# A new hand-written order of all steps in a fused sliding-window attention and expert kernel

## The chip, the cores and the metric

The kernel runs on one core of one Trainium2 chip. The metric is device time in microseconds (us). Before the change it was 203.53 us, the median of three runs (203.12 to 203.67).

## What is computed

Eight batches of eight heads go through causal attention with a window of 64 positions (576 positions, head dimension 64). The result, laid out as 576 rows of 512 per batch, goes through one of eight experts. The expert is chosen per batch from the mean of the batch's own attention output, so its weights cannot be fetched before that batch's attention is done.

```python
scores = scale * np.matmul(q, k.transpose(0, 1, 3, 2))
mask = (rel >= 0) & (rel < window)
scores = np.where(mask, scores, -1000000000.0)
...
x = np.ascontiguousarray(attn_out.transpose(0, 2, 1, 3)).reshape(B, S, H * D)
...
pooled = x.mean(axis=1)
logits = pooled @ w_gate
e_idx = np.argmax(logits, axis=1)
...
    h = np.maximum(x[mask] @ w1[e], 0.0)
    out[mask] = gate_w[mask, None, None] * (h @ w2[e])
```

## The kernel before

**Units.** Attention is cut into 40 units, five per batch: unit 5b+i with i below 4 is two heads by the first 512 positions of batch b, and unit 5b+4 is the last 64 positions of all eight heads (the tail). A unit goes through these steps, each one letter of the order, with the unit's number behind it:

- T (L214): 16 transposes on PE (8 for a tail) of q and then k, loaded as bf16, into one PSUM tile `tp`. A small m puts the tile into the pool `ps_m`, else it is in `ps_t`, which has one buffer.
- U and k (L238, L249): copies of the q half and of the k half out of PSUM into `qt` and `kT`. A small a puts the copy on ACT, a small d on DVE.
- S (L257): 16 small matmuls that give the scores. With m they go into two tiles of `ps_m`, else into the one tile of `ps_s`. With b, two mask matmuls (L269) come first and put -30000 outside the window, so that no mask is needed afterwards.
- E (L279): the exponential on ACT. It is one instruction for `ps_s` (L288) and two for `ps_m` (L291).
- K (L295): the mask as a multiplication on DVE, for units without b.
- l, n, R (L303, L347, L354): row sums on PE into the one buffer `lb`, then logarithm and exponential on ACT, which give the reciprocal.
- A and X (L318, L360): the product with v on PE, and the scaling on DVE into `xm`, which also sums for the gate.

**Batches.** Q (L104) loads q (even number) or k (odd number) of a batch; L (L137) loads one of five parts of v, t (L130) the tails of q and k, V (L148) copies v into a shifted form on DVE. g, j, G, H, I (L378 to L439) compute the gate; P (L411) reads the chosen expert's number into a register of POOL, and W (L416) loads one of four pieces of that expert's weights: 4b and 4b+1 are the halves of w1, 4b+2 and 4b+3 those of w2.

**Expert.** Each c takes the next of 18 chunks per batch: eight chunks of w1 (L461, 8 matmuls each), one for the tail rows (L470), eight half chunks of w2 (L503, 8 matmuls each) and one for the tail (L512). Chunk tiles share the three buffers of `ps_m` with the m variants above. ra and rd empty the next finished chunk on ACT or on DVE; O stores a finished output tile from POOL's queue, o from SP's (for a tail, half from SP's and half from ACT's, L492).

**What sets the order.** Nothing is scheduled automatically: the tuple OPS is a list of some 890 such letters, and each letter issues its instructions at that place on every engine that it touches. Each engine works through its own part strictly in that order. All loads and nearly all stores go through POOL's one queue, whose transfers land in the order of their issue. `ld` has three buffers for q and for k, `vw` three for v, and `w1b` and `w2b` three each (`WSLOT`, L98).

**The start.** Half of the heads of q and k of batch 0 come from POOL (heads 4 to 7 as "48", heads 0 and 1 as "02"), while heads 2 and 3 ("24") are loaded as float32 by SP (Y, L116) and cast on chip (C, L123).

```python
    with tc.manual_schedule():
        for op in OPS:
            c, x = op[0], op[1:].lstrip("abdm")
            e = op[1:len(op) - len(x)]
            if c == "c":
                todo.pop(0)()
            elif c in "oO":
                store(nc.sync if c == "o" else nc.gpsimd)
            elif c == "r":
                evac.pop(0)(e)
```

## Time and profile before

| | |
|---|---|
| time, median of three | 203.53 us |
| span of the profiled execution | 201.92 us |
| so around the span | 1.61 us |
| first transpose on PE | 6.88 us |
| first matmul of an expert (L461) | 40.84 us |
| last matmul issued (L512) | 196.54 us, a group of 16 |

The profiled execution is one run, and its own time outside the profiler is not told: its span and the 1.61 us that separate it from the median stand for it. All times below are counted from the span's start. A row of the timeline begins with start and duration; a row of the list of windows gives busy time per engine in that stretch; a row of the list of DMAs gives size and the time from issue to landing.

### The profile page before, as it was taken

How to read it: one execution, taken by the hardware profiler on the slowest of the kernel's cores; microseconds unless marked ns; L12 is line 12 of the kernel's file. 1: busy time of each engine (PE TensorE's matmuls, PEld its weight loads, DVE VectorE, ACT ScalarE, POOL GpSimd, SP SyncE). 2: the span in 40 equal slices, each digit the busy share in tenths (PEclk: the TensorE clock that was granted, in tenths of full speed). 3: DMA queues.
4: the chain of work that ended last, by engine and by line, in shares of the span. 5: the costliest groups of instructions: out<-in, count | busy, mean ns of one | idle time of the engine just before them, and what ended most of it. 6: DMA issues, size and time to landing. Idle time of an engine off the chain costs nothing.

```text
span 201.9 us, 8105 instructions
## 1 busy us (share of the span) xinstructions
PE 183.5 (91%) x3518; PEld 124.2 (62%) x3522; DVE 119.9 (59%) x347; ACT 131.8 (65%) x247; POOL 111.0 (55%) x158
## 2 busy tenths in 40 slices
PE   0487886899999999999999999999999999999991
PEld 0455564656677756577667666676656666776760
DVE  3527989595477546895877457966494651216410
ACT  2179998876599578977779975757787436321121
POOL 7985939235931593478633552439452716553561
PEclk9999999999999999999999999999999999999998
DMA  6999999999999999999999999999999999999693
GB/s 135 175 188 159 194 162 198 199 198 174 196 201 197 170 198 193 174 201 167 200 206 200 169 195 223 259 208 137 183 237 243 266 254 212 274 212 301 235 325 134
DMA packets 83346, 41.16 MB, mean 204 GB/s; under 512 B 48080, under 2 KB 80976, under 8 KB 83312
## 3 DMA queue, kind: packets, MB, share of 16 engines
q0 software_dynamic: 81936, 39.72, 138.5%
q1 hardware_dynamic: 768, 0.85, 1.3%
q8 instruction: 27, 0.44, 0.8%
q10 hardware_dynamic: 608, 0.08, 0.2%
q14 instruction: 7, 0.06, 0.1%
HBM read 61.88 MB, written 9.44 MB: 353 GB/s over the span
## 4 chain that ended last, share of the span: by engine, by line
PE 77%; DMA 9%; POOL 7%; issue 3%; DVE 2%; ACT 1%; POOLq 0%; DVEq 0%; ACTq 0%
PE ph L461 28%; PE po L503 25%; DMA vw<-in_v_dram 9%; PE tp L225 5%; PE ph L470 4%; PE s L275 4%; PE av L331 3%; PE po L512 3%; PE lb L309 3%; POOL vw L141 2%; POOL km L110 2%; POOL qm L110 1%; POOL out_dram L492 1%; PE gps L392 1%; POOL qkt L133 1%
## 5 line engine op out<-in xcount | busy, mean ns | idle before, releaser
L503 PE MATMUL po<-w2b,hm 128*64 128x512 f16 x512 | 60.1, 379 | 0.0
L461 PE MATMUL ph<-xm,w1b 128*64 128x512 f16 x512 | 60.0, 379 | 0.0
L461 PEld LDWEIGHTS <-w1b 128*64 128x64 f16 x512 | 31.7, 110 | 18.7 <-issue 0.4
L503 PEld LDWEIGHTS <-hm 128*64 128x64 f16 x512 | 30.1, 110 | 19.3
L141 POOL DMA_DIRECT2D vw<-in_v_dram x32 | 28.9, 910 | 13.3 <-DMA w1b<-in_moe_w_dram 4.3
L446 ACT ACTIVATE hm<-ph,gw 128x512 f16<-128x512 f32 x39 | 26.6, 693 | 13.4 <-PE ph L461 13.3
L492 POOL DMA_DIRECT2D out_dram<-ob x31 | 17.2, 557 | 25.0 <-DMA w1b<-in_moe_w_dram 7.0
L351 ACT ACTIVATE ln<-lb 128x512 f32<-128x512 f32 (+1 forms) x40 | 22.5, 563 | 11.8 <-PE lb L309 8.6
L364 DVE CUSTOM_DVE_ANT_0 xm<-av,rl 128x512 f16<-128x512 f32 x32 | 21.6, 686 | 10.4 <-PE av L331 9.5
L482 ACT COPY ob<-po 128x512 f32<-128x512 f32 x18 | 10.6, 586 | 23.6 <-PE po L503 23.6
L448 DVE TENSOR_SCALAR hm<-ph,gw 128x512 f16<-128x512 f32 x25 | 18.7, 748 | 12.1 <-PE ph L461 11.6
L357 ACT ACTIVATE rl<-ln 128x512 f32<-128x512 f32 (+1 forms) x40 | 23.3, 594 | 1.5 <-DVE pool L364 1.3
L225 PE MATMUL tp<-ident,qm 128*64 128x128 bf16 x256 | 13.8, 232 | 7.4 <-DMA qm<-in_q_dram 6.9
L288 ACT ACTIVATE pe<-s 128x1024 f16<-128x1024 f32 x19 | 19.5, 1028 | 1.4 <-PE s L275 0.7
L297 DVE TENSOR_TENSOR pe<-pe,mask 128x1024 f16<-128x1024 f16 x24 | 16.3, 687 | 3.9 <-ACT pe L288 3.1
L252 ACT COPY kT<-tp 128x512 bf16<-128x512 bf16 x19 | 11.2, 597 | 9.0 <-PE tp L225 8.0
L225 PEld LDWEIGHTS <-qm 128*64 128x64 bf16 x256 | 10.7, 118 | 10.0 <-DMA qm<-in_q_dram 6.9
L482 DVE COPY ob<-po 128x512 f32<-128x512 f32 x14 | 9.7, 690 | 10.7 <-PE po L503 10.5
L423 POOL DMA_DIRECT2D w1b<-in_moe_w_dram x16 | 12.6, 785 | 5.9 <-DMA vw<-in_v_dram 2.9
L275 PEld LDWEIGHTS <-kT 64*128 64x128 bf16 x576 | 10.1, 95 | 8.9 <-issue 5.6
L331 PEld LDWEIGHTS <-vw 128*64 128x64 f16 x512 | 12.4, 112 | 4.7 <-issue 1.2
L225 PE MATMUL tp<-ident,km 128*64 128x128 bf16 x256 | 13.9, 231 | 1.4 <-DMA km<-in_k_dram 0.9
(80 smaller groups left out, 267.2 us busy)
## 6 DMA issues: line engine op xcount, KB each, us to landing
w1b<-in_moe_w_dram POOLq DMA_DIRECT2D x16, 512.0 KB, 9.3
w2b<-in_moe_w_dram POOLq DMA_DIRECT2D x16, 512.0 KB, 13.4
out_dram<-ob POOLq DMA_DIRECT2D x31, 256.0 KB, 8.1
vw<-in_v_dram POOLq DMA_DIRECT2D x32, 128.0 KB, 9.0
km<-in_k_dram POOLq DMA_DIRECT2D x7, 512.0 KB, 9.3
qm<-in_q_dram POOLq DMA_DIRECT2D x7, 512.0 KB, 9.0
out_dram<-obt POOLq DMA_DIRECT2D x14, 64.0 KB, 7.7
qkt<-in_q_dram POOLq DMA_DIRECT2D x8, 64.0 KB, 7.6
```

The source lines that it names most:

```text
L141: nc.gpsimd.dma_start(out=vt[:, 2 * J + 1], in_=v[b, :, 128 * J:128 * J + 128].rearrange("h c d -> c h d"))
L225: nc.tensor.transpose(tp[p0:p0 + 64, n, r], t[:, 2 * i + hh, ts(r, 64)], ident)
L288: nc.scalar.activation(out=po, in_=sp[0], func=AF.Exp, scale=scale)
L351: nc.scalar.activation(out=ln, in_=lb[:, 0:n], func=AF.Ln)
L357: nc.scalar.activation(out=rl, in_=lns.pop((b, i)), func=AF.Exp, scale=-1.0)
L364: nc.vector.tensor_tensor_reduce(out=xm[:, i], in0=av.rearrange("q r p -> q (r p)"), in1=rl, scale=1.0, scalar=0.0, op0=ALU.mult, op1=ALU.add,
L446: nc.scalar.activation(out=o, in_=i, func=AF.Relu, scale=g)
L448: nc.vector.tensor_scalar(out=o, in0=i, scalar1=g, scalar2=0.0, op0=ALU.mult, op1=ALU.max)
L461: nc.tensor.matmul(out=ph[64 * c:64 * c + 64], lhsT=w1t[:, kb, ts(2 * ft + c, 64)], rhs=xm[:, kb], start=(kb == 0), stop=(kb == 3), skip_g ...
L482: copy(e)(out=ob, in_=po)
L492: (nc.scalar if n and eng is nc.sync else eng).dma_start(out=dst, in_=src)
L503: nc.tensor.matmul(out=po[64 * c:64 * c + 64], lhsT=hm[:, fb, ts(2 * r + c, 64)], rhs=w2t[:, fb], start=(fb == 0), stop=(fb == 7), skip_gr ...
```

## The change

Only the tuple OPS is replaced; no function changes. The file gets one line shorter, so that every line number falls by one (L461 becomes L460). The first line of the tuple, before and after:

```diff
-    "Y0.24 Q0.48 Q1.48 Q0.2 Cd0.24 y i Q1.2 Y1.24 Q3 Cd1.24 z Tm3 Tm2 mb T0 Tm1 ka3 ka2 ka0 "
+    "Q1.48 i Q0.48 Y1.24 Y0.24 T3 Q2 Ca1.24 t0 Cd0.24 y Tm2 mb Ua3 Tm1 kd3 kd2 Ud1 Q0.2 Ua2 Sm3 "
```

The same steps are done, with these differences in kind. Score tiles in `ps_m` fall from 16 units to 8, so that 8 pairs of half exponentials become single ones. 10 units instead of 9 use the mask matmuls, and the multiplications K fall from 31 to 30. Copies of k on ACT and DVE go from 20 and 20 to 16 and 24, copies of q from 9 and 31 to 14 and 26. Chunks are emptied 57 times on ACT and 55 on DVE, where it was 65 and 47. Five stores instead of two leave from SP's queue: all those of the last batch.

Place one is POOL's queue at the start of the program, before the change: qm and km are the q and k tiles, qkt the tails, `128x4x256` four heads, `128x2x256` two and `128x8x256` all eight.

```order
L110 DMA qm<-in_q_dram 128x4x256
L110 DMA km<-in_k_dram 128x4x256
L110 DMA qm<-in_q_dram 128x2x256
L181 ISA
L181 AFFINE_SELECT mt<-mt 128x64
L183 AFFINE_SELECT mt<-mt 128x64
L177 AFFINE_SELECT ident<-ident 128x128
L110 DMA km<-in_k_dram 128x2x256
L110 DMA km<-in_k_dram 128x8x256
L133 DMA qkt<-in_q_dram 64x8x64
L133 DMA qkt<-in_k_dram 64x8x64
L110 DMA qm<-in_q_dram 128x8x256
```

The same place after the change:

```order
L109 DMA km<-in_k_dram 128x4x256
L176 ISA
L176 AFFINE_SELECT ident<-ident 128x128
L109 DMA qm<-in_q_dram 128x4x256
L109 DMA qm<-in_q_dram 128x8x256
L132 DMA qkt<-in_q_dram 64x8x64
L132 DMA qkt<-in_k_dram 64x8x64
L180 AFFINE_SELECT mt<-mt 128x64
L182 AFFINE_SELECT mt<-mt 128x64
L109 DMA qm<-in_q_dram 128x2x256
L109 DMA km<-in_k_dram 128x2x256
L109 DMA km<-in_k_dram 128x8x256
```

The k half comes first and the identity matrix is built between it and the q half; all of batch 1's q and the first tails now stand ahead of heads 0 and 1 of batch 0.

Place two is DVE from the second half of the first shift of v (L151, batch 0) on, before: tp is a transposed PSUM tile, xm the scaled output, kT_95 the k tiles of batch 1.

```order
L151 COPY vw_91<-vw_91 64x4x512
L242 COPY qt<-tp 128x512
L364 ISA xm,pool<-av,rl 128x512
L364 ISA pool 128x1
L246 COPY qtt<-tpt 128x256
L242 COPY qt<-tp 128x512
L364 ISA xm,pool<-av,rl 128x512
L364 ISA pool 128x1
L364 ISA xm,pool<-av,rl 128x512
L364 ISA pool 128x1
L297 TENSOR_TENSOR pe<-pe,mask 128x1024
```

And after:

```order
L150 COPY vw_91<-vw_91 64x4x512
L241 COPY qt<-tp 128x512
L251 COPY kT_95<-tp 128x512
L363 ISA xm,pool<-av,rl 128x512
L363 ISA pool 128x1
L251 COPY kT_95<-tp 128x512
L363 ISA xm,pool<-av,rl 128x512
L363 ISA pool 128x1
L241 COPY qt<-tp 128x512 x2
L363 ISA xm,pool<-av,rl 128x512
L363 ISA pool 128x1
L251 COPY kT_95<-tp 128x512
```

Three full k copies of batch 1 now stand among the scalings that lead to the first gate; before the change the k copies of batch 1 were on ACT or ahead of the shift.

Place three is PE where the first expert chunk (ph) begins, before: km_820 is the k of batch 3, tp_1085 the PSUM tile of unit 16.

```order
L225 LDWEIGHTS km_820
L225 MATMUL tp_1085<-ident_105,km_820 64x128
L461 LDWEIGHTS w1b0_96
L461 MATMUL ph_1106<-xm_489,w1b0_96 64x512
L461 LDWEIGHTS w1b0_96
```

After, at the start of the chunk (al_1058 is the product with v of unit 9) and, in the second fence, at its end:

```order
L338 LDWEIGHTS vw1_92
L338 MATMUL al_1058<-pp_906,vw1_92 64x64
L460 LDWEIGHTS w1b0_96
L460 MATMUL ph_1070<-xm_433,w1b0_96 64x512
L460 LDWEIGHTS w1b0_96
```

```order
L460 LDWEIGHTS w1b0_96
L460 MATMUL ph_1070<-xm_433,w1b0_96 64x512
L224 LDWEIGHTS qm_740
L224 MATMUL tp_1085<-ident_105,qm_740 64x128
L224 LDWEIGHTS qm_740
```

Ahead of the first chunk PE has 256 transposes of the L225 kind before the change and 224 after it: the transposes of units 16 and 18 have moved behind it. All other PE work ahead of it is the same, but for one pair of mask matmuls more (16 became 18 of the full size).

## Prediction

> **What bounds the kernel now.** I read the page first, for the engines' shares and the 40 slices of 5 us each.

> ```profile
> PE 183.5 (91%) x3518; PEld 124.2 (62%) x3522; DVE 119.9 (59%) x347; ACT 131.8 (65%) x247; POOL 111.0 (55%) x158
> PE   0487886899999999999999999999999999999991
> DMA  6999999999999999999999999999999999999693
> ```

> PE is full from slice nine on and has holes before it. The DMA row is at its top from the second slice to nearly the end, so the transfers are a second resource without slack. The list of windows says the same in numbers.

> ```profile
> 13.00:41.00 28.00, 22.13 (x603) 15.78 (x606) 20.76 (x61) 25.77 (x50) 18.34 (x24) 1.00 1.77 184
> 41.00:197.00 156.00, 155.91 (x2831) 104.23 (x2827) 94.15 (x268) 101.61 (x193) 80.94 (x115) 1.00 1.40 213
> ```

> From 13 to 41 us ACT (the fourth number with a count) works 25.8 of 28 us and PE 22.1. From 41 to 197 us PE works 155.9 of 156 while ACT and DVE have a third of their time free. So there are two stages, and what divides them is the first expert chunk. From there PE always has a chunk that it can do, and the end comes as soon as PE's remaining work is done. A change of order can gain in three ways only: start the first chunk earlier, leave less work behind it, or shorten what follows the last matmul. The chain of waits shows what the first chunk waited for.

> ```profile
> 22.68 8.52 DMA vw<-in_v_dram
> 31.32 0.88 DVE vw L150
> ...
> 40.56 0.45 PE tp L225 x16
> 41.01 4.32 PE ph L461 x40
> ```

> The chain runs through the last v of batch 1 and its shift, and then through steps of attention that end with the transposes of unit 16. The chunk did not wait for its weights, as the timeline of POOL and the list of DMAs show.

> ```profile
> 27.82 0.88 POOL L110 DMA_DIRECT2D km<-in_k_dram  x1 [1.72 <-DVE grd L384]
> 30.04 0.75 POOL L423 DMA_DIRECT2D w1b<-in_moe_w_dram  x1 [1.34 <-DVE kT L252]
> 30.78 0.89 POOL L141 DMA_DIRECT2D vw<-in_v_dram  x1
> km<-in_k_dram POOLq DMA_DIRECT2D x1, 512.0 KB, 9.0
> w1b<-in_moe_w_dram POOLq DMA_DIRECT2D x1, 512.0 KB, 9.4
> vw<-in_v_dram POOLq DMA_DIRECT2D x1, 128.0 KB, 9.5
> 40.84 1.46 PE L461 MATMUL ph<-xm,w1b 128*64 128x512 f16 x12
> ```

> Issue plus time to landing gives 36.8 for k of batch 3, 39.4 for the first quarter of weights and 40.3 for the v transfer behind it. So 512 KB take 2.6 us of the queue and 128 KB about 0.86, and each follows the one before it without a gap. PE begins the chunk at 40.84, 1.4 us after its weights are there. These 1.4 us are the most that an earlier start can bring, since the weights come from a queue that is already full.

> **The change, part by part.** First, the transfers ahead of the first weights. Counted in the order of POOL, 26 transfers stand ahead of them before the change and the same 26 after it, in another sequence. A full queue that moves the same bytes ends at the same time, so the weights land at 39.4 again, if the queue stays full. Two places could break that. At the start the identity matrix is built between the first two transfers.

> ```profile
> 4.49 0.29 POOL L177 TENSOR_SCALAR_AFFINE_SELECT ident<-ident 128x128 bf16<-128x128 bf16 x1
> qm<-in_q_dram POOLq DMA_DIRECT2D x1, 256.0 KB, 5.4
> km<-in_k_dram POOLq DMA_DIRECT2D x1, 256.0 KB, 6.0
> 6.88 0.64 PE L225 MATMUL tp<-ident,qm 128*64 128x128 bf16 x8 [6.88 <-DMA qm<-in_q_dram]
> 8.41 0.64 PE L225 MATMUL tp<-ident,km 128*64 128x128 bf16 x8 [0.89 <-DMA km<-in_k_dram]
> ```

> That delays the second transfer by 0.3 us, up to 0.4 with the gaps around it. The second landed 1.5 us after the first, and nothing says that a later issue slows it while the first still moves: between 0 and 0.4 us, and I take 0.15, nearer to nothing because the queue is backed up. PE's first transposes need q first, which is now the second half to land, so PE starts at about 8.5 and not at 6.9. Only the q transposes of one unit (8 of them) lose that lead; the k half was waited for until 8.41 anyway. A later transfer sets the pace again before long (k of batch 1 with heads 0 to 7 of q ahead of it), so I count nothing for it.

> The second place is the gate of batch 0, which must be known before the weights are issued. Between the first shift of v and the gate, DVE gets three k copies, a tail k copy and one q copy more and one multiplication K less.

> ```profile
> L252 DVE COPY kT<-tp 128x512 bf16<-128x512 bf16 x4 | 2.7, 681 | 0.7 <-PE tp L225 0.7
> L242 DVE COPY qt<-tp 128x512 bf16<-128x512 bf16 x9 | 3.7, 415 | 1.9 <-PE tp L225 1.9
> L297 DVE TENSOR_TENSOR pe<-pe,mask 128x1024 f16<-128x1024 f16 x1 | 0.7, 693 | 0.1
> ```

> The tail copy has half the width, so about 0.3. That is 3 x 0.68 + 0.3 + 0.42 - 0.69 = 2.1 us, so the weights are issued at 32.1 and not at 30.04, when DVE has no free time to absorb it. Q and K of batch 3 and a small v tail are ahead of them in the queue and keep it busy to about 37. A transfer issued at 32.1 has 7.3 us to land by 39.4. The program's first one, 256 KB onto an empty queue, took 5.4 us; with 1.3 us for the other 256 KB that makes 6.7, so that anything issued by 32.7 is on time. The margin is 0.6 us.

> Is PE ready at 39.4? The last q of batch 3 now lands as the last big one before the weights, near 36.5. Behind it PE does the transposes of units 17 and 15 (0.45 each), two pairs of row sums, one masked score step and a tail product: about 2.3 us, so 38.8. ACT's list between its first exponential and the chunk is as long as before to a few tenths: one pair of halves more for one whole exponential less, two k copies less and one q copy more. DVE's list from the shift to the chunk is the same within half a microsecond, since what it does earlier is missing later. ACT begins earlier, because its first exponential stands behind two q copies and no longer behind four k copies.

> ```profile
> L252 ACT COPY kT<-tp 128x512 bf16<-128x512 bf16 x5 | 3.0, 616 | 0.0
> ```

> Two copies fewer at that place are 1.2 us. I take the start of the chunk at 39.6: weights at 39.45 plus 0.15. **First term: 39.6 - 40.84 = -1.24 us**, with ends -1.4 (weights alone) and +2.1 (all of DVE's added work arrives at the chunk).

> Second, the work behind the first chunk. Two full sets of transposes (units 16 and 18, 32 instructions) have moved behind it. The chain's row of 16 transposes costs 0.45 us on a full PE, and there PE has nothing to hide it under. **Second term: +0.90 us.**

> Third, one more pair of mask matmuls, ahead of the chunk.

> ```profile
> 36.46 0.54 PE s L269 x2
> ```

> It is 0.54 us of PE in a stretch where PE idles 5.9 of 28 us: nothing, or 0.54 if PE became the limit there.

> Fourth, the weights behind the first quarter. Two v transfers instead of one stand between the first and second quarter: it lands at 39.45 + 2 x 0.86 + 2.6 = 43.8. PE needs it after four chunks, a unit of transposes, one score step and a gate matmul (0.2), at 39.6 + 3.45 + 0.45 + 0.34 + 0.2 = 44.0. On time by 0.2 us. Later weights have over a microsecond each by the same sum of queue times. Nothing, but the margin is thin.

> Fifth, the end. The last batch's stores move from POOL to SP.

> ```profile
> 197.65 0.37 ACT L487 COPY obt<-po 128x256 f32<-128x256 f32 x1 [0.29 <-PE po L512]
> out_dram<-ob POOLq DMA_DIRECT2D x1, 256.0 KB, 2.7
> out_dram<-ob SPq DMA_DIRECT2D x1, 256.0 KB, 3.2
> out_dram<-obt ACTq DMA_DIRECT2D x1, 64.0 KB, 2.6
> ```

> The last full tile (ready at 197.4) would land near 200.6 from SP, when the last tail half lands at 198.05 + 2.6 = 200.65. Zero, or +0.3 if the tail half on SP queues behind it; I take zero. [...]

> Moving work from ACT to DVE behind the first chunk costs nothing by itself: both have over 50 us free there.

> **Sum:** 201.92 - 1.24 + 0.90 = 201.58 us of span, and with the 1.61 us around it 203.2 us. That is 0.3 us less than the median, under the 0.3% (0.6 us) that a measurement of this kernel can tell from no change.

> **Rivals.** *DVE becomes the bound of the first stage* (slower). The 2.1 us that stand ahead of the gate also push back the second shift of v and the copies behind it, and PE waits there. Against it: DVE works 20.8 of the 28 us. For it: the chain above runs through exactly that shift. It decides against the change when the chunk begins after 40.84 - 0.90 = 39.94. With 0 to 2.1 us on the start it gives 201.92 + 0.90 + 0 to 2.1 + 1.61 = 204.4 to 206.5. [...] The granted clock is 1.00 in both windows before the change, so I give such a wait 0.03 out of this rival's chance.

> *Weights come late* (slower). Transfers are not all alike in pace.

> ```profile
> vw<-in_v_dram POOLq DMA_DIRECT2D x1, 128.0 KB, 13.7
> w2b<-in_moe_w_dram POOLq DMA_DIRECT2D x1, 512.0 KB, 16.7
> 52.02 0.98 POOL L141 DMA_DIRECT2D vw<-in_v_dram  x1
> 52.99 0.76 POOL L426 DMA_DIRECT2D w2b<-in_moe_w_dram  x1
> ```

> Here the one landed at 65.7 and the next at 69.7: 4.0 us for what takes 2.6 elsewhere. Such a loss of 1.4 us in the first weights exceeds the 0.2 us of margin and gives 203.2 + 1.2 = 204.4.

> *The second stage gets denser* (faster). The chain has what each kind of PE work takes when nothing holds it up.

> ```profile
> 68.66 0.34 PE s L275 x16
> ...
> 72.52 0.22 PE lb L309 x2
> ...
> 75.78 0.25 PE av L331 x16
> ```

> With 0.86 per chunk of 8 expert matmuls and 0.45 per unit of transposes, the work behind 40.84 adds up to about 155.1 us, and it takes 156.6. If these 1.5 us of small gaps shrink to between half and nothing, because ACT has eight pairs of halves and eight evacuations less, it gives 203.2 - 0.75 to 1.5 = 201.7 to 202.4.

> *The order does not matter*: the same first chunk time, as other waits take the place of those removed, plus the two transposes, is the low end of the first rival, 204.4.

> **How the numbers follow.** Forecast 0.36 (202.6 to 203.8), DVE bound 0.30, late weights 0.10, denser 0.24. Faster by over 0.3% is below 202.92: all of the denser case and a quarter of the forecast's, 0.33. Slower is above 204.14: the DVE case and 0.06 of the late weights, 0.36. The rest, 0.31, is no change. The range leaves a tenth out at each end: 201.9 to 205.6.

> **What would show it.** The first matmul of L460 at 39.5 to 39.9 with the weights' landing just ahead of it shows the first term right; a start after 40.2 with the weights landed shows DVE or ACT as the bound. The first gate matmul near 30 instead of 28 shows the 2.1 us. PE busy 156.5 of the 157 us that follow shows the second term and the margins. The forecast is wrong if PE waits for w1b or w2b anywhere, if the weights land at another time than 39.4 to 39.8, or if the time from the last matmuls' start (196.54) to the end is not 5.4 us.

## The result, and the profile after

The changed kernel takes 213.14 us (median of four runs, 209.82 to 215.81) where before takes 203.32 in the same comparison (203.05 to 203.67). The ratio is 1.0368, with a 95% interval of 1.03 to 1.0437: slower, outside the range predicted. The ratio is made from 209.82 and 212.28 alone; the other two runs, the profiled one (214.01) among them, count as disturbed.

The page of after, first its busy line, then three rows of its 40 slices (5.3 us each), as the page of before was read:

```profile
PE 189.0 (89%) x3524; PEld 133.6 (63%) x3524; DVE 126.3 (59%) x352; ACT 125.2 (59%) x233; POOL 109.3 (51%) x155
...
PE   0489896799999997998899999998899999999992
...
PEclk9999997999999999999999999999999999999999
DMA  7999999999999999999995999999994999799995
```

PE now has holes behind slice nine, where before had a row of nines, and its clock row has a 7. The windows, split at the first expert chunk (43.2 us, last matmul at 208.3; columns as in the prediction):

```profile
13.00:43.20 30.20, 25.28 (x589) 17.35 (x590) 21.40 (x63) 24.35 (x48) 20.55 (x25) 0.94 1.78 179
43.20:208.30 165.10, 159.38 (x2877) 113.07 (x2874) 100.06 (x273) 96.82 (x181) 77.95 (x112) 1.00 1.31 200
```

Before started the chunk at 40.8 and needed 156.5 us from there to its last matmul (156.41 of them busy). After needs 165.1. So of the 10.5 us between the two profiled executions 2.4 lie ahead of the first chunk, 8.6 behind it, and -0.5 behind the last matmul (4.1 us to the end for 4.6). The ratio gives a loss of 7.5 us; the 10.5 belong to this one execution. Now the rows of PE's timeline that carry an idle time "<-issue", that is, one for which no semaphore answers:

```profile
34.96 0.64 PE L330 MATMUL av<-pe,vw 128*64 128x64 f16 x16 [0.97 <-issue]
...
41.16 0.36 PE L224 MATMUL tp<-ident,km 128*64 128x128 bf16 x6 [1.17 <-issue]
...
81.35 0.38 PE L231 MATMUL tpt<-ident,qkt 128*64 128x128 bf16 x7 [1.33 <-issue]
...
101.48 0.22 PE L330 MATMUL av<-pe,vw 128*64 128x64 f16 x2 [1.64 <-issue]
...
149.60 0.29 PE L274 MATMUL s<-qt,kT 64*128 64x64 bf16 x8 [1.62 <-issue]
...
172.12 1.91 PE L502 MATMUL po<-w2b,hm 128*64 128x512 f16 x15 [0.42 <-issue]
```

They break off inside a unit, once between two identical transposes of one tile. No data dependence lies there. Four of them, 5.0 us, are behind the first chunk. What they have in common is their distance, in the windows from one stall's end to the next (the number after x is the count of matmuls, then of weight loads):

```profile
34.95:41.15 6.20, 5.02 (x128) 3.82 (x128) 4.84 (x14) 4.40 (x9) 5.55 (x7) 0.76 1.55 175
41.15:81.34 40.19, 38.41 (x767) 25.00 (x767) 27.23 (x77) 29.32 (x54) 20.04 (x25) 1.00 1.46 180
81.34:101.47 20.13, 18.48 (x383) 12.29 (x382) 12.43 (x33) 14.37 (x30) 11.87 (x16) 1.00 1.73 185
101.47:149.59 48.12, 46.25 (x894) 29.69 (x894) 30.94 (x86) 31.82 (x58) 20.65 (x28) 1.00 1.34 184
149.59:172.11 22.52, 22.10 (x383) 13.25 (x383) 14.95 (x41) 13.01 (x24) 11.07 (x18) 1.00 1.14 201
```

128, 767, 383, 894 and 383 are 1, 6, 3, 7 and 3 times 128, less one or two (semaphore instructions stand between). A matmul and its weight load are two instructions, so the stalls fall on multiples of 256 PE instructions. The page's DMA part has a queue of just that kind, in both kernels alike:

```profile
q8 instruction: 27, 0.44, 0.8%
```

```
matmuls     entered  packet starts  next piece starts  work in it  stall
1243-1371     74.72      78.99           81.35            5.30     1.33
1371-1499     81.35      85.36           88.15            6.80     none
1626-1754     97.26      99.10          101.48            2.57     1.64
2521-2648    143.67     147.23          149.60            4.30     1.62
2903-3031    165.98     169.10          172.12            5.72     0.42
```

A stalled piece goes on 2.3 to 2.4 us after its packet starts (3.0 in the last row, where the packet itself took 1.6 us instead of 0.9), and in the four stalled rows the packet starts 1.8 to 4.3 us after PE entered the piece ahead: 4.2 to 6.6 us in all. The one stall of 0.50 us in the chain of before, at 38.68, is of this kind too (packet at 36.23). In the changed kernel such a stall costs up to 1.64 us a piece.

### The profile page after: what moved, and what is told of

Its sections match the earlier page's. It is cut to its first block, busy times and chain, and to the rows that moved or that the text cites. A ratio compares the mean times of both kernels' runs of the same rounds, so it can differ in the third digit from the quotient of the medians.

```text
span 212.4 us, 8119 instructions
## 1 busy us (share of the span) xinstructions
PE 189.0 (89%) x3524; PEld 133.6 (63%) x3524; DVE 126.3 (59%) x352; ACT 125.2 (59%) x233; POOL 109.3 (51%) x155
## 3 DMA queue, kind: packets, MB, share of 16 engines
q1 hardware_dynamic: 1200, 1.64, 2.3%
## 4 chain that ended last, share of the span: by engine, by line
PE 79%; ACT 8%; issue 5%; DVE 3%; DMA 3%; POOL 1%; POOLq 0%; DVEq 0%
PE po L502 27%; PE ph L460 25%; PE s L274 5%; PE tp L224 5%; PE av L330 4%; PE ph L469 4%; PE po L511 3%; PE lb L308 3%; DMA qm<-in_q_dram 3%; ACT ln L350 2%; ACT kT L251 1%; ACT rl L356 1%; ACT pe L287 1%; PE s L268 1%; PE tpt L231 1%
## 5 line engine op out<-in xcount | busy, mean ns | idle before, releaser
L460 PE MATMUL ph<-xm,w1b 128*64 128x512 f16 x512 | 60.8, 380 | 0.5 <-ACT kT L251 0.5
L460 PEld LDWEIGHTS <-w1b 128*64 128x64 f16 x512 | 34.2, 110 | 15.8 <-issue 0.4
L502 PEld LDWEIGHTS <-hm 128*64 128x64 f16 x512 | 33.6, 110 | 15.2 <-issue 0.9
L447 DVE TENSOR_SCALAR hm<-ph,gw 128x512 f16<-128x512 f32 x38 | 28.1, 748 | 19.3 <-PE ph L460 18.7
L287 ACT ACTIVATE pe<-s 128x1024 f16<-128x1024 f32 x26 | 26.7, 1026 | 7.8 <-PE s L274 6.5
L491 POOL DMA_DIRECT2D out_dram<-ob x28 | 15.5, 557 | 22.1 <-DVE hm L447 5.2
L481 ACT COPY ob<-po 128x512 f32<-128x512 f32 x21 | 12.3, 586 | 22.7 <-PE po L502 22.7
L445 ACT ACTIVATE hm<-ph,gw 128x512 f16<-128x512 f32 x26 | 17.7, 690 | 12.9 <-PE ph L460 12.8
L425 POOL DMA_DIRECT2D w2b<-in_moe_w_dram x16 | 12.2, 768 | 20.0 <-PE av L330 13.3
L330 PE MATMUL av<-pe,vw 128*64 128x64 f16 x512 | 14.9, 199 | 3.8 <-issue 2.6
L274 PE MATMUL s<-qt,kT 64*128 64x64 bf16 x512 | 14.1, 197 | 2.7 <-issue 1.6
## 6 DMA issues: line engine op xcount, KB each, us to landing
w1b<-in_moe_w_dram POOLq DMA_DIRECT2D x16, 512.0 KB, 9.2
w2b<-in_moe_w_dram POOLq DMA_DIRECT2D x16, 512.0 KB, 11.5
out_dram<-ob POOLq DMA_DIRECT2D x28, 256.0 KB, 7.8
vw<-in_v_dram POOLq DMA_DIRECT2D x32, 128.0 KB, 9.1
qm<-in_q_dram POOLq DMA_DIRECT2D x7, 512.0 KB, 10.3
km<-in_k_dram POOLq DMA_DIRECT2D x7, 512.0 KB, 8.6
out_dram<-ob SPq DMA_DIRECT2D x4, 256.0 KB, 3.2
```

Source lines behind the costliest of these rows:

```text
L274: nc.tensor.matmul(out=sp[hh][:, ts(m, 64)], lhsT=kq, rhs=qt[p0:p0 + 64, m], start=not pm, stop=True, skip_group_check=True)
L287: nc.scalar.activation(out=po, in_=sp[0], func=AF.Exp, scale=scale)
L330: nc.tensor.matmul(out=av[p0:p0 + 64, :, 16 * m:16 * m + 16], lhsT=vt[:, m, 2 * i + hh], rhs=pe[:, hh, m], start=(m == 0), stop=(m == 7), ...
L445: nc.scalar.activation(out=o, in_=i, func=AF.Relu, scale=g)
L447: nc.vector.tensor_scalar(out=o, in0=i, scalar1=g, scalar2=0.0, op0=ALU.mult, op1=ALU.max)
L460: nc.tensor.matmul(out=ph[64 * c:64 * c + 64], lhsT=w1t[:, kb, ts(2 * ft + c, 64)], rhs=xm[:, kb], start=(kb == 0), stop=(kb == 3), skip_g ...
```

## The experiments

| run | us, median (n) | ratio to before, 95% |
|---|---|---|
| changed kernel | 213.14 (4) | 1.0368 (1.030 to 1.0437) |
| before + 28 idle matmuls | 207.65 (4) | 1.0193 (1.0168 to 1.0219) |
| before + 128 | 203.73 (10) | 1.0018 (0.9993 to 1.0042) |
| changed, chunks shifted | 218.05 (4) | 1.0695 (1.0623 to 1.0766) |
| changed, wide expert matmuls | 218.14 (5) | 1.0699 (1.066 to 1.0738) |
| changed, second stage reordered: first / mended | 209.59 (4) / 208.94 (4) | 1.0294 (1.0231 to 1.0358) / 1.0233 (1.0156 to 1.031) |
| changed, fewer weight loads | 210.29 (4) | 1.0345 (1.0288 to 1.0402) |
| changed + 128 idle matmuls | 210.40 (4) | 1.0313 (1.0226 to 1.0399) |
| new head, rest of before ("mixed") | 208.22 (6) | 1.0215 (1.0154 to 1.0275) |
| head of before, new rest | 215.05 (4) | 1.0523 (1.045 to 1.0596) |
| mixed, v shift early | 208.56 (4) | 1.0238 (1.0167 to 1.0308) |
| mixed, q first | 208.20 (4) | 1.0198 (1.0155 to 1.0241) |
| mixed, copies as before | 207.20 (4) | 1.0168 (1.0123 to 1.0214) |
| before, k first | 203.54 (12) | 0.9989 (0.9969 to 1.0009) |
| before, copies as after | 203.78 (12) | 1.0003 (0.9981 to 1.0025) |
| before, last stores on SP | 203.35 (12) | 0.9988 (0.996 to 1.0015) |
| before / mixed, moved by the replay | 204.86 (10) / 208.82 (4) | 1.0056 (1.0021 to 1.009) / 1.0276 (1.0191 to 1.0361) |

### Moving the boundaries without touching the order

```
-    "Y0.24 Q0.48 Q1.48 ...
+    "F28 Y0.24 Q0.48 Q1.48 ...      (and F128 in the second run)
-  nc.tensor.matmul(out=wps, lhsT=warm[:, 0:128], rhs=warm, ...)
+  nc.tensor.matmul(out=wps[0:64, 0:64], lhsT=warm[:, 0:64], rhs=warm[:, 0:64], ...)
```

> The kernel before with 28 idle matmuls (64 columns) ahead of PE's first transposes, where PE waits for q anyway. Theory A (PE's instructions are fetched in pieces of 256, that is 128 matmuls with their weight loads; a piece is asked for when PE enters the one ahead of it and is there 5.0 to 5.8 us later, so a piece that PE works off in less ends in a stall that no semaphore shows): every boundary stands 28 matmuls earlier in the program, on denser pieces; a replay of the trace of before with 5.6 us per piece sums to 5.9 us of stalls where it sums to 1.6 with the boundaries as they are, so 206.5 to 208.5 us. Theory B (the stalls of the changed kernel belong to places of its order: late data or buffers that the profile does not name): the order is that of before, so 203.0 to 203.9 us and no new gaps.

> The kernel before with 128 of the same idle matmuls ahead of the first transposes: one whole piece, so the boundaries stand where they stood. Theory A: 203 to 204.5 us (the idle matmuls may reach to 8.3 us and hold up the first transposes a little) and PE's gaps as before. Theory B: the same 203 to 204.5. With the run of 28 it tells a shift of the boundaries from the mere presence of idle matmuls: if those cost time by themselves, this run is slower than that of 28.

28 idle matmuls cost 1.9%, 128 of them nothing that can be told from zero. PE's waits behind the first chunk with 28 (line waited for, us, times, longest), and the windows between the ends of its stalls:

```profile
PE po L502 <- issue: 1.6, 1, 1.6
PE s L274 <- issue: 1.1, 1, 1.1
PE ph L460 <- issue: 0.6, 1, 0.6
PE av L330 <- issue: 0.6, 1, 0.6
```

```profile
38.56:44.48 5.92, 5.33 (x128) 3.79 (x128) 4.87 (x18) 4.99 (x9) 2.25 (x3) 1.00 1.40 200
44.48:96.72 52.24, 51.68 (x1023) 34.53 (x1023) 34.25 (x95) 39.19 (x75) 28.92 (x36) 1.00 1.61 181
96.72:121.56 24.84, 23.74 (x511) 15.95 (x511) 16.91 (x48) 19.86 (x38) 12.57 (x17) 1.00 1.55 194
```

An order that had no such stall behind its first chunk now has four, 3.9 us, and the ends shown lie 1, 8 and 4 pieces of 128 matmuls apart. With 128 idle matmuls none is left there. That shows the core of theory A, that these stalls go by the count of instructions, and refutes theory B for them: the order of the steps is the same in both runs and in before. No run moved the boundaries of the changed kernel by part of a piece, so how much of its 5.0 us is its order and how much the place of the boundaries in it stays open.

### Repairing the changed kernel's second stage

The first try moved only chunks and evacuations against the attention steps, by their PE work alone; here the piece that stalled at 101 us:

```
-rd L26 l21 L24 c ra L25 V4 S26 n21 ra A20 Ua29 ... K26 T27 Am23 ... l22 R23 c R24
+L26 l21 L24 L25 V4 S26 n21 A20 c c c rd c ra ra Ua29 ... K22 c K26 T27 Am23 ... R24
```

> The changed kernel with the expert chunks and their evacuations behind the first chunk shifted by a few steps against the steps of attention, so that no piece of 256 PE instructions has too little work; head, loads, transfers' order and engines are unchanged. Theory A: the stalls of 1.33, 1.64, 1.62 and 0.42 us (5.0 us) fall below 1.2 us together: 207.5 to 209.5 us. Theory B: the same waits at much the same places, 211.5 to 214 us.

The time rose to 218. The stalls were gone, as meant, but PE waited elsewhere for real data; these are its largest waits behind the first chunk:

```profile
PE s L274 <- ACT pe L287: 2.2, 3, 0.9
PE al L338 <- DVE pool L363: 1.9, 1, 1.9
PE av L330 <- DVE pool L363: 1.0, 2, 0.8
```

The chunks had covered ACT's and DVE's latencies where they stood. The expectation was wrong in the time. It is no test of theory A, since it traded one kind of wait for another. The next tries ordered the steps behind the seventh chunk by a replay of the program that I made from durations and latencies in these traces; it knows both kinds of wait.

```
-S26 n21 ra A20 Ua29 rd l24 X20 L28 L27 P3 c ka29 E26 K22 K26 T27 Am23 kd27 n24 l22 R23 c
+A20 S26 c l21 c c L25 L24 n21 rd rd Ua29 l24 rd X20 L28 c L27 ka29 E26 P3 K22 T27 K26 n24
```

> The changed kernel with its head untouched up to the seventh chunk, and the steps behind it put in another order by a replay that knows the latencies of ACT and DVE, the queue of POOL, and a piece of 256 PE instructions 5.4 to 6.0 us after the one ahead was entered. Without the pieces that replay gives the same time for this order as for the changed kernel's (198.4 and 198.3 us), with them 198.7 and 204.3. Theory A: the stalls behind the first chunk fall from 5.0 to under 1 us, and the time to 203.5 to 208 us, with the head's loss left in it. Theory B (late data that the profile does not name): no gain, 211 to 215 us, since the same work waits on the same engines.

> The changed kernel with its head untouched up to the seventh chunk and the steps behind it in another order, as in the run before of this kind, but with every mask multiplied in ahead of the steps that read it (that run had some behind them, so that a part of its output was unmasked). The replay that orders it knows the pieces of 256 PE instructions. Without the pieces it gives 198.1 us here and 198.3 for the changed kernel, with them 198.7 and 204.3. Theory A: no stall over 0.5 us without a releaser behind the first chunk; 206 to 209.5 us, the head's loss left in it. Theory B: 211 to 215 us.

Both came out near or within theory A's figures (209.59, a little above its 208; 208.94, inside). Besides the order, both put copies (19 and 23 of 80) on the other engine and 5 and 6 more evacuations on ACT, so they don't test the order alone. In the mended run PE's waits behind the first chunk are these two and no more:

```profile
PE ph L460 <- ACT kT L251: 0.4, 1, 0.4
PE s L274 <- issue: 0.3, 1, 0.3
```

The pieces that stalled in the changed kernel (at 1371, 1754, 2648 and 3031) now hold about 6.2, 6.4, 6.2 and 5.7 us of work instead of 5.30, 2.57, 4.30 and 5.72. From the first chunk to the last matmul it takes 159.7 us for 165.1. By the ratios the repair gives 1.35% back, 2.7 us, though the two intervals just touch; the head's loss stays. That is less than the 5.0 us of stalls in the profiled execution of the changed kernel; their size varies: at the same four matmuls two other kernels with this rest and all its loads show 3.6 and 3.0 us. A third way to thin the pieces is to halve the instructions of the expert chunks:

```
-for c in range(2):
-    nc.tensor.matmul(out=ph[64 * c:64 * c + 64], lhsT=w1t[:, kb, ts(2 * ft + c, 64)], ...)
+nc.tensor.matmul(out=ph, lhsT=w1t[:, kb, ts(ft, 128)], ...)      (and so for po and the tail)
```

> The changed kernel with expert matmuls over 128 columns of the weights in place of two over 64: half as many PE instructions in each chunk (about 5400 in all for 7071), the same arithmetic. Theory A: with half the instructions per chunk no piece of the second stage is worked off in under 5.8 us except where attention stands alone, so at most 1.5 us of its 5.0 us of stalls are left: 207 to 210 us if a chunk still takes 0.86 us. If the wider weight loads no longer hide (0.11 us each for 64 columns), a chunk grows by up to 0.4 us and the time by some 50 us; then only the gaps can be read, not the time. Theory B: the stalls stay at their places, 212 to 214 us at an unchanged pace.

No stall is left behind the first chunk, as theory A has it, and yet it is slower. PE's timeline shows why (four wide matmuls are one chunk):

```profile
165.47 1.04 PE L459 MATMUL ph<-xm,w1b 128*128 128x512 f16 x4
166.43 0.41 PE L231 MATMUL tpt<-ident,qkt 128*64 128x128 bf16 x8
```

A chunk between attention steps takes 0.96 us where eight narrow matmuls took 0.86. A wide weight load takes 98 ns, a narrow one in the changed kernel 110; no run shows the reason for the longer chunk. This profile also has 6.8 us at half the clock around its first chunk (45.5 us; a 7 and a 6 in the clock row of its 5.5 us slices).

### What the pieces wait for

```
-... E27 E28 W12 A22 Q12 Q13 S25 W13 ...
+... E27 E28 A22 Q12 Q13 S25 ...        (W12 to W31 all left out)
```

> The changed kernel without the weight loads of batches 3 to 7 (20 of 32 transfers of 512 KB; these batches use the weights that lie in the buffers from batches 0 to 2, so their output is not the reference's). All PE instructions stay, and so do the boundaries. Theory A1 (a piece of instructions comes late because its packet waits among the transfers of the software queue): where the queue has thinned out, from about 75 us on, a piece starts under 2 us after it is asked for, and not 3 to 5 us; the stalls at matmuls 1754, 2648 and 3031 (1.64, 1.62, 0.42 us) go, the one at 1371 (79 us) may stay: 208.5 to 210.5 us. Theory A2 (a piece takes its 5.5 us whatever else is moved): the stalls stay, 211.5 to 214 us.

The DMA row of its slices (5.2 us each) shows that the queue thinned out from 104 us on only, not from 75:

```profile
DMA  6999999999999999999903990099304800795023
```

Ahead of that the stall at 1754 stayed (1.92 us) and the one at 1371 shrank to 0.48. Behind it packets start 1.3, 0.3 and -0.2 us after the pieces ending at 2648, 3031 and 3159 were entered, and the stalls at 2648 and 3031 are gone. The one at 3031 is absent from two runs with all loads too (the other mix and the changed kernel with 128 idle matmuls, both below); the one at 2648 is in both, with 1.11 and 1.02 us, so it is the one that counts: that piece, worked off in 4.21 us, no longer stalls. Of the 12 packets from 106 us to the last piece, ten start within 1.3 us of PE's entry into the piece ahead, some before it. That speaks for theory A1, with the wrong time for the point where it begins: a packet of instructions starts later while POOL's queue is full, in the changed kernel at a median of 3.5 us after the entry. The time doesn't show it: the median of 210.29 is within A1's figure, but its interval overlaps that of the changed kernel.

### The head

> The new order up to the seventh expert chunk, then the order of before, stores of the last batch on POOL as before. Theory A (PE's instructions come in pieces of 256, a piece is there about 5.5 us after PE entered the one ahead, and pieces with too little work stall): the second stage is that of before with boundaries moved by a few matmuls, so its stalls stay under 1.5 us; the time from the first chunk to the end is that of before (161 us) to +1.5. What is left of the loss is the later first chunk of the profile (43.2 for 40.8): 203.5 + 0 to 3 = 203.5 to 206.5 us. Theory C (the head of the order makes nearly the whole loss, and the later stalls only follow from it): 211 to 214 us.

> The order of before up to the seventh expert chunk, then the new order with its stores on SP; R11 and E15 are put a few steps later, which the change of head asks for. Theory A: the first chunk starts at 40.8 as before, and the stalls in the second stage come at the same dense places, some 5 us in a replay of it: 206.5 to 209.5 us. Theory C: 203 to 204.5 us.

The seams: R10 and L14 are set at the first one, R12, R11 and E15 at the second; the second mix also leaves out one unit's mask (0.7 us of DVE).

```
+... K11 R12 j1 c c c T16 G1 H1 ra L14 R10 | rd l14 K13 c t3 ra c P1 ...    (new | before)
+... ra ra c H1 L10 c | R12 l11 V2 rd rd n11 Ud16 c A12 L16 Q8 ...          (before | new)
```

The mixed order came to 208.22 (206.48 to 210.11), above theory A's figure and below theory C's. Behind the first chunk its PE waits only once, 0.2 us for ACT, and takes 157.7 us to its last matmul: 156.5 of before plus the two transposes. So the second stage's loss belongs to the new rest. The head costs 2.15% by the ratio, 4.4 us. The profiled execution, the fastest of the six, shows 3.0 of them: 0.8 at the first chunk (41.68), 1.2 in the second stage, mostly the transposes, and 0.9 behind the last matmul (5.5 us to the end for 4.6). That last part isn't the stores: they land 3.3 us behind the last matmul in both, and what fills the rest is not shown. The other mix took 215. It has the stalls of the new rest, at the same matmuls (0.65, 1.79, 1.11 us), but also waits of 3.8 us for a shift of v that its own seam made late, and 6.8 us at half the clock behind that (an 8 and a 5 in the clock row of its 5.4 us slices); it tells nothing on the head.

> The changed kernel with 128 idle matmuls ahead of its first transposes, one whole piece, so that the boundaries stay: it warms the array before the first q is there. Theory D (half the clock until 17.3 us, and again for 3.4 us near 35, is what delays the first chunk): full clock from about 5 us on gives 1.5 to 3 us back, the first chunk starts at 40 to 41.5, and the time is 209 to 212 us. Theory A alone: the first stage is held by pieces of 256 instructions that take 5.5 us each whatever the clock, so the first chunk moves by under 1 us and the time stays at 211.5 to 214.5 us.

The edit is F128 ahead of the new order. Theory D's time came, 210.40, with an interval that overlaps that of the changed kernel, and nearly its first chunk (41.7 for 40 to 41.5). When q came, eight transposes took 0.22 us and no longer 0.43; 0.22 is what they take in the changed kernel at 29 us, at a granted clock of 1.00. But the half clock returned for 3.4 us, as in the changed kernel (granted clock 0.91 from 21.68 to 41.72 us); the stalls in the head were absent, and those behind it were 0.32, 1.65 and 1.02 us. It doesn't separate clock and pieces. In the trace of the changed kernel the clock's fall at 34.5 us looks like this (the last three numbers of a row are the granted clock, the DMA share and GB/s):

```profile
27.60:31.10 3.50, 3.29 (x90) 2.48 (x88) 2.10 (x14) 3.50 (x7) 0.27 (x1) 1.00 1.92 177
31.10:34.50 3.40, 1.73 (x44) 1.35 (x43) 3.29 (x10) 2.64 (x8) 1.21 (x2) 0.99 1.48 198
```

```profile
34.70:38.10 3.40, 3.14 (x74) 2.44 (x75) 2.17 (x7) 2.53 (x6) 3.40 (x5) 0.53 1.23 171
```

Ahead of the fall, in a stretch as long as the fall itself, PE was busy for 1.73 of 3.4 us, and then it ran at half clock for 3.41 us, by that share an estimated 1.7 us lost. In the mixed order 3.4 us with 1.72 busy came ahead of the same fall, at 21.8 (granted clock 0.50 from there to 25.2). But such a stretch does not always do it: the mixed order with q first, below, was busy for 1.44 us of the 3.41 from 30.94 on, and before for 1.74 of those from 31.34 on, and both kept the clock. So no threshold can be read from these runs.

> The mixed order of before (new head up to the seventh chunk, then the order of before), with the shift of batch 1's v on DVE put ahead of the gate of batch 0 (right behind g0) and no longer behind G0. In the run without this edit the shift ended at 34 us although its v had landed by 29.6, and the first chunk began at 41.7. Theory E (the shift stands behind the gate on DVE, and the first chunk hangs on the shift): the shift ends near 32, 2 us earlier, and the first chunk begins at 39.8 to 40.6; 1 to 2 us less than the run without the edit. Theory F (the gate and with it the first weights set the first chunk, so DVE's 1.4 us ahead of the gate only move the wait): the weights land 0.7 to 1.4 us later and the first chunk begins at 41.5 to 42.5: no gain.

```
-g0 ka12 Q6 Ud12 j0 Ud10 Sb12 G0 V1 R5 H0
+g0 V1 ka12 Q6 Ud12 j0 Ud10 Sb12 G0 R5 H0
```

The shift moved as meant, from 32.9 to this (DVE's timeline), and the first chunk came at 43.39, no earlier; the time did not fall.

```profile
30.63 0.69 DVE L149 COPY vw<-vw 64x2048 f16<-64x2048 f16 x1 [0.25 <-DMA vw<-in_v_dram]
31.33 0.69 DVE L150 COPY vw<-vw 64x2048 f16<-64x2048 f16 x1
```

Theory E falls. F's later chunk was seen (weights landed at 41.1 instead of 40.0), but stalls of 0.64 and 0.66 us and a stretch at half the clock are in it too (granted clock 0.92 from 22.23 to 43.39 us). Now the parts of the head one by one, in before and in the mixed order:

```
-"Y0.24 Q0.48 Q1.48 Q0.2 Cd0.24 y i       +"Y0.24 Q1.48 i Q0.48 Q0.2 Cd0.24 y       (before, k first)
-"Q1.48 i Q0.48 Y1.24                     +"Q0.48 Q1.48 i Y1.24                     (mixed, q first)
-ka3 ka2 ka0 ... Ud3 Ud2 ... ka5 ... ka6  +kd3 kd2 kd0 ... Ua3 Ua2 ... kd5 ... kd6  (before; mixed the other way)
```

> The order of before with one part of the change alone: k's half of batch 0 is loaded first, the identity matrix is built behind it, and q's half comes second. Theory G (the start costs: PE can begin only with q, 1.3 us later, and the first stage has no slack to take that up): PE starts at 8.2 to 8.5 and not at 6.9, the first chunk begins 0.6 to 1.5 us later, 204.1 to 205.1 us. Theory H (a full queue of transfers sets the pace again within some us): 203.3 to 203.9 us.

> The mixed order with q's half of batch 0 loaded first, then k's, then the identity matrix. Theory G: PE starts 0.5 to 1.4 us earlier than 8.4 and the first chunk comes 0.5 to 1.4 us earlier: 206.8 to 207.7 us. Theory H: 207.8 to 208.6 us as the mixed order (208.2).

> The order of before with the engines of the copies ahead of the gate of batch 0 as the new order has them: six more k copies and a tail's on DVE (units 0, 1, 2, 3, 5, 6, 9), one k copy (unit 4) and three q copies (units 2, 3, 7) on ACT. Theory I (DVE becomes the bound of the first stage: what stands ahead of the gate and the second shift of v delays both): the gate's matmul 0.6 to 2 us later than 28.0, the first chunk 0.6 to 2 us later, 204.1 to 205.6 us; a replay gives +0.64. Theory J (DVE has the time free): 203.3 to 203.9 us.

> The mixed order (new head up to the seventh chunk, then before's) with those copies on the engines that before uses: the edit of the run before this one, the other way round. Theory I: DVE reaches the gate of batch 0 up to 2 us earlier, the first chunk comes 1 to 2 us earlier: 206 to 207.3 us, where the mixed order took 208.2. Theory J: 207.7 to 208.7 us; ACT, with six copies more, can make it slower (the replay says +1.3, 209.5).

Loading k first costs nothing (203.54, theory H), though PE starts at 8.26 and not at 6.88; q first brings nothing back (208.20, H). In that second run PE starts two microseconds earlier, and then stalls in the same head:

```profile
6.27 0.64 PE L224 MATMUL tp<-ident,qm 128*64 128x128 bf16 x8 [6.27 <-DMA qm<-in_q_dram]
```

```profile
40.55 0.36 PE L224 MATMUL tp<-ident,km 128*64 128x128 bf16 x6 [1.76 <-issue]
```

Six more k copies on DVE cost nothing either (203.78, theory J): the gate's matmul came at 28.5 where before had 28.0. In its profiled execution the first chunk came at 41.68, behind 3.4 us at half the clock (mean granted clock of the run 0.991); the median shows no loss. The other way round gave 207.20, one microsecond below the mixed order with overlapping intervals: undecided. What the heads share is their pace from the end of the wait for batch 0's v, at 22 us in all of them, to the first chunk. Before, and the mixed order with q first, where the clock was full throughout:

```profile
22.26:40.84 18.58, 14.58 (x436) 11.04 (x440) 14.73 (x49) 16.82 (x33) 11.65 (x15) 1.00 1.69 188
```

```profile
21.54:42.63 21.09, 15.67 (x442) 11.66 (x448) 15.22 (x50) 17.60 (x35) 13.72 (x18) 1.00 1.69 184
```

That is 3.4 pieces at 5.5 us each and 3.45 at 6.1, at about what a piece takes to come (4.2 to 6.9 us after the entry where PE stalled in the changed kernel). But the pieces don't pace the whole head. Eleven profiles have the new head, each with at most one change in it. In five (the mixed order, with copies as before too, and the changed kernel with chunks shifted, with fewer loads, with 128 idle matmuls) no stall "<-issue" over 0.2 us comes from 22 us to the first chunk, and it starts at 41.65 to 41.96. In the other six there are stalls of 1.0 to 3.0 us in sum, at the same one or two boundaries, and it starts at 42.6 to 45.5. So one head comes out in two ways, and the stalls, with the half clock that comes with most of them, go with the part above some 42 us. Where the first microsecond (41.7 for 40.84) comes from is not shown: the mixed order with copies as before has it without a stall and at full clock.

### Two orders from the replay, and the stores

```
-"Y0.24 Q0.48 Q1.48 Q0.2 Cd0.24 y i Q1.2 Y1.24 Q3 ...    +"Y0.24 Q1.48 Q0.48 Cd0.24 Q0.2 Q1.2 y i Y1.24 ...
-"Q1.48 i Q0.48 Y1.24 Y0.24 T3 Q2 Ca1.24 ...             +"Q1.2 Y0.24 Q1.48 i Q0.48 L0 Y1.24 Q0.2 Cd0.24 ...
-ra rd o O c ra O c ra o                                 +ra rd o o c ra o c ra o
```

> The order of before, with steps moved by few places by the same replay with pieces (steps move by 0 to some 10 places; stores of the last batch as before). The replay gives 197.3 us for it and 203.5 for before, 6.1 us less: 2.1 from an earlier first chunk and 4 from the second stage. By theory A and the replay: 198 to 201 us. If the head is set by what the replay does not know (the array's clock, late transfers), the second stage alone gains: 200 to 203 us. If the replay's waits are not the chip's: 203 to 208 us.

> The mixed order (new head, then the order of before), all of it moved freely by the same replay with pieces of PE instructions; in the replay 197.1 us for 203.3. Theory A with the replay: 198 to 201 us. If the head is set by what the replay does not know: 201 to 205 us. If the replay's waits are not the chip's: 205 to 212 us.

> The order of before with the last five stores on SP, as the new order has them, where before has three of the five on POOL. The prediction costed this at 0 (or +0.3): 203.3 to 203.9 us. Theory K (POOL's queue ends the kernel later than SP's does): from the last matmul to the end the profiles show 4.58 us for before and 4.06 for the changed kernel, so 0.5 us less: 202.8 to 203.2 us.

The replay's orders did not gain: 204.86 (0.2 to 0.9% slower than before) and 208.82. Both also have 35 copies on another engine. Neither has a stall of pieces behind the first chunk. But the chunk came at 41.3 and 40.8, no earlier than in before, where the replay had a gain of 2.1 us for the first, and in the second PE waited 2.2 us for data later on. The replay comes within 2 us for before (203.5 for a span of 201.9); on the two orders that it chose it was 6 and 9 us too low (197.3 and 197.1 for 203.3 and 206.0). With the last stores on SP the end lies 4.06 us behind the last matmul where before had 4.58, but the time (203.35) can't be told from no change. No version here beats before.

## Why the prediction was wrong, point by point

**Two steps failed.** The first is: "From there PE always has a chunk that it can do, and the end comes as soon as PE's remaining work is done." PE had the work, but not always the instructions; the sum has no term for that, and it cost 5.0 us in the profiled execution. The profile of before showed the one stall that could have warned, in the middle of 8 like transposes, and I passed over it:

```profile
38.68 0.38 PE L225 MATMUL tp<-ident,km 128*64 128x128 bf16 x7 [0.50 <-issue]
```

In before, the pieces came in time but for that one stall of 0.50 us, and with 28 idle matmuls ahead of them it took 1.9% longer. The shortest piece behind the first chunk holds 2.57 us of work in the changed kernel and about 5.0 in before. My replay gives 198.3 us for the changed kernel without pieces and 204.3 with them; that is a calculation, and on other orders it was far off. I had called a denser second stage the faster rival; its short pieces are what stalls.

The second is in the first term: "Behind it PE does the transposes of units 17 and 15 (0.45 each), two pairs of row sums, one masked score step and a tail product: about 2.3 us, so 38.8." That takes PE to be waiting for the last q of batch 3. It was not: when that q landed, at 35.74, PE still had 162 matmuls ahead of the chunk, 6.3 us of work in the changed kernel, part of it at half clock, and 154 with 5.35 us in the mixed order, which had no stall there. So the term of -1.24 us became +2.4 in the changed kernel and +0.8 in the mixed order.

- *First chunk at 39.6.* The weights landed 0.7 us earlier than I said (38.72 for 39.4), but PE was not ready: 43.24. The two stalls ahead of it are 2.1 us, the half clock up to an estimated 1.7 (half of 3.41); both overlap with other waits.
- *Gate near 30, weights issued by 32.7.* The gate's matmul came at 30.55, near the figure by luck: I had counted copies on DVE, and these alone move it by 0.5 us (28.5). In the changed kernel PE didn't wait ahead of it. What moved it is PE's order: from the wait for batch 0's v to the gate PE works nearly all the time, through some 150 matmuls before and some 220 after the change. The two stretches, before and after:

```profile
22.26:28.02 5.76, 4.93 (x147) 3.44 (x148) 5.15 (x22) 5.65 (x11) 3.76 (x6) 1.00 1.92 177
22.07:30.55 8.48, 7.82 (x219) 5.67 (x220) 7.04 (x26) 8.00 (x14) 4.25 (x6) 1.00 1.90 178
```

The weights were issued at 33.29, too late by my margin, and still landed in time, because POOL had issued nothing for 5.4 us and the queue had run thin (down to 51 GB/s at 35.3 us):

```profile
33.29 0.76 POOL L422 DMA_DIRECT2D w1b<-in_moe_w_dram  x1 [5.42 <-DVE vw L149]
```

- *Two transposes, 0.90.* About right: the mixed order takes 157.7 us behind the first chunk for 156.5, with 0.2 us of named wait. In front they saved nothing: 38 matmuls fewer stand ahead of the wait for batch 0's v, which ends near 22 us in both heads, and 8 more between it and the first chunk.
- *k first 0.15, mask pair 0, weights in time 0.* Right as far as tested. k first measured -0.3 to +0.1%; in the changed kernel none of PE's waits behind the first chunk names a transfer. No run has the mask pair alone.
- *Stores 0.* Right in the time; in the profile half a microsecond better.
- *The rival "DVE becomes the bound"* had the right sign, but not the size (204.4 to 206.5) and not the cause: its copies alone change nothing (203.78), and the shift set free did not help.
- *A wait of PE that halves its clock* had 0.03. Half the clock came at the first chunk or ahead of it in nine of twelve profiles with the new head, the replay's order among the twelve (mean granted clock 0.984 to 0.992 in the nine, 0.997 to 1.000 in the other three), and in two with the old one (0.987 with 128 idle matmuls, 0.991 with the copies as after). No run shows how long such a wait has to be or that a wait alone brings it. What the runs showed is that in the changed kernel and the mixed order no gap ahead of the fall was over 1.0 us and PE was busy for 1.73 and 1.72 of 3.4 us, while in the mixed order with q first a stretch of 3.41 us with 1.44 us of work did not bring it.

Of the profiled 10.5 us, 5.0 are stalls behind the chunk, 0.9 transposes, 0.7 named waits, 2.0 more busy time of PE there, 2.4 the later chunk, -0.5 the end. What stays open is that busy time, how the head's 2.4 divide between pieces, clock and the rest, and how the 7.5 us of the ratio divide: by it the new head alone costs 4.4.

## What to carry to other kernels

Where a busy engine stops with "<-issue" in the middle of like instructions, count instructions between such stops. In this kernel they were multiples of 256, and each stop in the changed kernel ended 2.3 to 2.4 us (3.0 once) after a 16 KB packet had started on the queue of kind "instruction". In the changed kernel a block that PE had to wait for came 4.2 to 6.9 us after it entered the one ahead, under a full DMA queue. A stretch of short matmuls worked off in 2.57 us stalled there for 1.64 us, and 28 idle matmuls ahead of before moved its blocks and brought four stalls behind the first chunk. And where a step is forecast to follow a transfer, count the work that the engine still has in front of it when the transfer lands.

## What the runs showed of the hardware

- 27 packets of 16 KB on the queue of kind "instruction" go with some 7070 PE instructions, and PE's stalls stand multiples of 256 instructions apart. In the changed kernel, under a full queue of POOL, a packet starts up to 4.6 us after PE enters the block ahead (median 3.5); where the queue was thin, ten of 12 start within 1.3 us of it, some before. PE, where it stalls, goes on 2.3 to 2.5 us after the packet starts (3.0 once).
- PE's granted clock fell to 0.50 for 3.4 us (3.41 in the changed kernel) behind 3.4 us in which PE was busy for 1.73 us (changed kernel) and for 1.72 us (mixed order), with no gap over 1.0 us; in the mixed order with q first it stayed at 1.00 behind a stretch of 3.41 us with 1.44 us of work.
- Expert matmuls with 128 columns of weights take 0.96 us a chunk between attention steps, two with 64 each 0.86.
- The last matmul is followed by 4.06 us with the last stores on SP and by 4.58 with three of five on POOL; in the mixed order, with the same stores, by 5.5.
